# VectorE's attention as a hardware loop of eight trips, with ring slots freed by two VectorE operations

## The chip, the cores and the metric

The kernel runs on one core of one Trainium2 chip. The metric is the device time in microseconds (us) of one execution; times are medians of the fast ones among several executions. Each execution is labelled fast or slow. Slow ones take 444 to 447 us here, and one execution of the kernel before took 888.3 us; they are left out wherever two kernels are compared.

## The reference

It is one decode step of a transformer block with adaptive layer norm, batch 8, one new token per sequence. Attention has 32 query heads on 4 key/value heads, a cache of 8192 positions and head size 128. A gated MLP (1024 to 3584 to 1024) follows.

```python
mod = (_silu(c) @ w_mod).reshape(8, 6, 1, -1)          # sa, ca, ga, sb, cb, gb
h = _layernorm(x) * (1 + ca) + sa
q = (h @ wq).reshape(B, 1, Hq, Dh).transpose(0, 2, 1, 3)
scores = einsum('bhqd,bhkd->bhqk', q, repeat(k_cache)) * Dh ** -0.5
o = einsum('bhqk,bhkd->bhqd', softmax(scores), repeat(v_cache))
x = x + ga * (o.reshape(B, 1, Hq * Dh) @ wo)
h = _layernorm(x) * (1 + cb) + sb
gate, up = h @ W_gate, h @ W_up
return x + gb * ((gate * (gate > 0) * up) @ W_down)
```

The key and value caches are 134 MB of the 185.6 MB that have to be read. Each of these bytes has to be read once, so the reading itself is the natural limit.

## The kernel before

Everything from HBM goes through one ring in SBUF of 128 KB per partition. K and V of one attention step (two of the 32 batch-and-group pairs) take 4 MB each, so four such loads fill the ring: K m, V m, K m+1, V m+1. SyncE issues the loads in a fixed order, each as soon as the readers of what it overwrites are done. A small recorder turns declared reads and writes into semaphore waits.

```python
def pump():
    while stream:
        key, src, n = stream[0]
        lo = cursor[0] if cursor[0] + n <= RING else 0
        if P.unread("arena", lo, lo + n):
            return
        ...
        P.op("sp", lambda e, dst=dst, src=src: e.dma_start(dst, src), writes=[slot_r(lo, lo + n)], dma=True,
             own=("v", key[1] % 2) if key[0] == "v" else None)
```

One attention step: VectorE transposes K in 8 parts (`kt_part`), TensorE multiplies (`qk_part`), VectorE finds the row maxima and folds the previous step's output, ScalarE takes the exponential, VectorE transposes P (`p_turn`), TensorE multiplies by V (`pv`). `qk_part` also declares a read of K's slot that it does not need, so a K slot is freed by TensorE; a V slot is freed by `pv`, TensorE again.

```python
def kt_part(m, e8):
    ...
    P.op("dve", lambda e: e.transpose(ktb[:, to:to + QE].bitcast(dt.uint32), arena[:, lo:lo + QE].bitcast(dt.uint32)),
         reads=[slot_r(lo, lo + QE)], writes=[R("kt", to, to + QE)])

def qk_part(m, e8):
    ...
    P.op("pe", fns, reads=[R("kt", to, to + QE), R("qpad", m % 2, m % 2 + 1), slot_r(place["k", m] + e8 * QE, ...)],
         writes=[bank(b)])

def fold(m, i):
    if m < 0:
        if i == 3:
            P.op("dve", lambda e: e.memset(om[:], 0.0), writes=[R("om")])
        return
    ...
for m in range(M):                     # M = 16
    P.trip = m // 2
    for e8 in range(8):
        kt_part(m, e8)
        qk_part(m, e8)
        if e8 == 5:
            rowmax(m, 0)
    make_qpad(m + 2)
    fold(m - 1, 0); fold(m - 1, 1)     # (joined lines)
    rowmax(m, 1)
    spread(m)
    fold(m - 1, 2)
    headmax(m)
    expo(m)
    fold(m - 1, 3)
    fold_pe(m - 1)
    ...
    p_turn(m)
    pv(m)
```

TensorE's part is already a hardware loop of 8 trips of two steps. Since the body of the loop is the same code in each trip, it cannot wait for ever growing counts; instead, each semaphore that it waits on is counted down by a fixed step at the end of a trip. VectorE's part is written out 16 times.

```python
with nc.Fori(0, len(self.trips), engines=(mybir.EngineType.PE,)):
    for p, limit in zip(self.trips[1], self.limit, strict=True):
        ...
        body(p, want)
    for s, v in self.step.items():
        e.wait_ge(sems[s], v).then_inc(sems[s], -v)
```

## Time and profile before

| What | Value |
|---|---|
| time, fast runs | 437.57 to 437.83 us |
| span of the profiled run | 436.2 us |
| bytes moved, mean rate | 185.79 MB, 426 GB/s |
| VectorE busy, instructions | 263.0 us (60%), 373 |

The page of the kernel before: its span, its busy times, the DMA rows of its 40 slices (tenths of busy time, then GB/s) and the DMA queues. Queue q1 carries the loads that SyncE issues; q8 and q14 carry instructions that engines fetch.

```profile
span 436.2 us, 4054 instructions
...
PE 273.5 (63%) x1697; PEld 124.0 (28%) x1697; DVE 263.0 (60%) x373; ACT 30.7 (7%) x65; POOL 20.9 (5%) x79
...
DMA  9999999999999999999999999999999999999995
GB/s 376 421 457 431 433 433 431 430 433 433 433 433 433 433 433 433 433 433 433 433 433 433 433 433 433 433 433 433 433 433 430 433 433 433 441 429 434 427 421 224
DMA packets 6939, 185.79 MB, mean 426 GB/s; under 512 B 816, under 2 KB 912, under 8 KB 1168
...
q1 hardware_dynamic: 6848, 185.63, 98.8%
q8 instruction: 6, 0.10, 0.1%
...
q14 instruction: 5, 0.04, 0.0%
```

The DMA row is 9 until the last slice, and the rate stays at 430 to 433 GB/s through the attention: the DMA engines that move data do not run dry there. (A 9 only says 90% or more; the steady rate says more.) Every compute engine is idle for a third of the time or more. The place to look for an effect is therefore whether a load is ever issued too late.

The groups of the page, K's transposes (count, busy us, mean ns; then VectorE's idle time just before them and what ended it), and the issues of the K and V loads (count, size, median us from issue to landing):

```profile
L539 DVE STREAM_TRANSPOSE kt<-arena 128x1024 uint32<-128x1024 uint32 x128 | 148.5, 1214 | 40.5 <-DMA arena<-in_A_k_cache_dram 37.9
...
arena<-in_A_k_cache_dram SPq DMA_DIRECT2D x16, 4096.0 KB, 27.5
arena<-in_A_v_cache_dram SPq DMA_DIRECT2D x16, 4096.0 KB, 25.6
```

VectorE waits 37.9 us for K to land, in 16 steps: 2.4 us a step of room. A load lands some 26 us after its issue though its transfer takes 9.7 us, so nearly two others are queued ahead of it.

SyncE's timeline before (start, duration of the issue, both in us):

```profile
73.23 0.33 SPq L343 DMA_DIRECT2D arena<-in_A_k_cache_dram  x1
85.56 0.33 SPq L343 DMA_DIRECT2D arena<-in_A_v_cache_dram  x1
93.25 0.33 SPq L343 DMA_DIRECT2D arena<-in_A_k_cache_dram  x1
```

VectorE's timeline in the same stretch of the kernel before, the two operations that will free slots among them:

```profile
89.15 0.69 DVE L558 TENSOR_REDUCE negm<-ps 128x1 f32<-128x512 f32 x1 [0.24 <-PE ps L550]
...
95.04 0.17 DVE L572 SCALAR_TENSOR_TENSOR mjt<-mj,jms 128x16 f32<-128x16 f32 x1
95.14 0.08 DVE L572 DVE_READ_ACCUMULATOR mjt<-mj,jms 128x1 f32 x1
```

### The profile page before, as it was taken

The page shows a single profiled execution, that of the slowest core. Times are in us where ns is not written, and L with a number is a line of the kernel's source. Part 1 is how long each engine was busy: PE and PEld are TensorE (multiplying, and loading weights), DVE is VectorE, ACT ScalarE, POOL GpSimd, SP SyncE. Part 2 cuts the span into 40 slices and gives each one's busy share as a digit, 9 for nine tenths or more (in the row PEclk, how much of TensorE's full clock was granted, in tenths as well). Part 3 has the DMA queues.
Part 4 walks back from the last instruction along what each step waited for, and adds up shares of the span by engine and source line. Part 5 has one row for each costly group of instructions (what it writes and reads, how often), then busy time and mean ns, then how long its engine had stood idle before and what let it go on. Part 6 is the DMA issues. An engine that isn't in the chain of part 4 may idle for free.

```text
span 436.2 us, 4054 instructions
## 1 busy us (share of the span) xinstructions
PE 273.5 (63%) x1697; PEld 124.0 (28%) x1697; DVE 263.0 (60%) x373; ACT 30.7 (7%) x65; POOL 20.9 (5%) x79
## 2 busy tenths in 40 slices
PE   0052447769595866859586775959586684655237
PEld 0021112324242332424233232423233231342015
DVE  0233057778596878778696877859686877332020
ACT  1100020010101011010101101010101101010000
POOL 7000010000000000000000000000000000000000
PEclk9996558698787989787896969879798978868568
DMA  9999999999999999999999999999999999999995
GB/s 376 421 457 431 433 433 431 430 433 433 433 433 433 433 433 433 433 433 433 433 433 433 433 433 433 433 433 433 433 433 430 433 433 433 441 429 434 427 421 224
DMA packets 6939, 185.79 MB, mean 426 GB/s; under 512 B 816, under 2 KB 912, under 8 KB 1168
## 3 DMA queue, kind: packets, MB, share of 16 engines
q1 hardware_dynamic: 6848, 185.63, 98.8%
q8 instruction: 6, 0.10, 0.1%
q10 hardware_dynamic: 80, 0.02, 0.0%
q14 instruction: 5, 0.04, 0.0%
HBM read 185.63 MB, written 0.02 MB: 426 GB/s over the span
## 4 chain that ended last, share of the span: by engine, by line
DMA 38%; PE 33%; DVE 20%; issue 8%; ACT 0%; SPq 0%
DMA arena<-in_A_k_cache_dram 25%; PE ps L594 13%; PE ps L550 12%; DVE kt L539 12%; DMA arena<-in_w_mod_dram 7%; DMA arena<-in_B_W_down_dram 6%; DVE negm L558 4%; PE ps L744 2%; PE ps L694 1%; PE ps L564 1%; PE ps L615 1%; DVE om L609 1%; DVE mj L569 1%; PE ps L725 1%; PE ps L463 1%
## 5 line engine op out<-in xcount | busy, mean ns | idle before, releaser
L539 DVE STREAM_TRANSPOSE kt<-arena 128x1024 uint32<-128x1024 uint32 x128 | 148.5, 1214 | 40.5 <-DMA arena<-in_A_k_cache_dram 37.9
L550 PE MATMUL ps<-kt,qpad 128*128 128x512 bf16 x512 | 122.0, 384 | 10.3 <-DVE kt L539 8.8
L594 PE MATMUL ps<-arena,pT 128*64 128x512 bf16 x512 | 92.0, 538 | 50.9 <-issue 50.9
L594 PEld LDWEIGHTS ps<-arena,pT 128*64 128x64 bf16 x512 | 44.2, 153 | 92.6 <-issue 86.7
L550 PEld LDWEIGHTS ps<-kt,qpad 128*128 128x128 bf16 x512 | 45.6, 97 | 85.2 <-DVE kt L539 29.6
L585 DVE STREAM_TRANSPOSE pT<-prb 64x1024 bf16<-64x1024 bf16 x32 | 39.7, 1239 | 16.8 <-ACT prb L578 16.3
L578 ACT ACTIVATE prb<-ps,bias 128x1024 bf16<-128x1024 f32 x16 | 17.8, 1114 | 286.5 <-DVE mjt L572 286.5
L558 DVE TENSOR_REDUCE negm<-ps 128x1 f32<-128x512 f32 x32 | 22.0, 688 | 11.3 <-PE ps L550 11.1
L532 POOL COPY qpad<-qR 32x32 bf16<-32x32 bf16 x64 | 13.0, 203 | 304.7 <-PE ps L550 252.0
L725 PE MATMUL ps<-arena,hT 128*32 128x448 bf16 x128 | 11.0, 515 | 13.6 <-DMA arena<-in_B_W_gate_dram 6.8
L564 PE MATMUL ps<-identf,negm 128*128 128x128 f32 x32 | 7.8, 326 | 15.6 <-DVE negm L562 15.6
L615 PE MATMUL ps<-jmp,om 128*128 128x16 f32 x34 | 6.7, 273 | 16.9 <-DVE om L609 16.1
L609 DVE SCALAR_TENSOR_TENSOR om<-ps,im,om 128x128 f32<-128x128 f32 x48 | 16.7, 347 | 0.6
L486 PE MATMUL ps<-arena,hT 128*32 128x512 bf16 x64 | 7.2, 631 | 14.1 <-DMA arena<-in_A_wq_dram 14.1
L732 DVE TENSOR_TENSOR kt<-ps,kt 128x448 bf16<-128x448 f32 x2 | 1.2, 620 | 23.5 <-PE ps L725 23.5
L744 PE MATMUL ps<-arena,hmT 128*32 128x256 bf16 x112 | 9.0, 332 | 5.3 <-DMA arena<-in_B_W_down_dram 5.3
L401 DVE CAST cxr<-ps 128x512 bf16<-128x512 f32 x1 | 0.7, 692 | 18.1 <-PE ps L399 18.1
L399 PE MATMUL ps<-cx,rsel 32*128 32x512 bf16 x1 | 0.6, 604 | 17.5 <-DMA cx<-in_c_dram 17.5
L564 PEld LDWEIGHTS ps<-identf,negm 128*128 128x128 f32 x32 | 4.7, 186 | 23.5 <-DVE negm L562 23.5
L496 DVE CAST kt<-ps 128x512 bf16<-128x512 f32 x1 | 0.7, 692 | 17.8 <-PE ps L486 17.8
L615 PEld LDWEIGHTS ps<-jmp,om 128*128 128x128 f32 x34 | 5.1, 188 | 20.3 <-DVE om L609 19.4
L725 PEld LDWEIGHTS ps<-arena,hT 128*32 128x32 bf16 x128 | 4.2, 128 | 20.1 <-DMA arena<-in_B_W_gate_dram 7.2
(89 smaller groups left out, 103.9 us busy)
## 6 DMA issues: line engine op xcount, KB each, us to landing
arena<-in_A_k_cache_dram SPq DMA_DIRECT2D x16, 4096.0 KB, 27.5
arena<-in_A_v_cache_dram SPq DMA_DIRECT2D x16, 4096.0 KB, 25.6
arena<-in_w_mod_dram SPq DMA_DIRECT2D x2, 6144.0 KB, 24.0
arena<-in_A_wq_dram SPq DMA_DIRECT2D x2, 4096.0 KB, 31.1
arena<-in_A_wo_dram SPq DMA_DIRECT2D x2, 4096.0 KB, 26.9
arena<-in_B_W_gate_dram SPq DMA_DIRECT2D x2, 3584.0 KB, 23.6
arena<-in_B_W_up_dram SPq DMA_DIRECT2D x2, 3584.0 KB, 24.6
arena<-in_B_W_down_dram SPq DMA_DIRECT2D x1, 3584.0 KB, 25.5
```

Of the source, the lines that this page charges most:

```text
L532: P.op("pool", lambda e, n=2 * m + Q // 2, Q=Q: e.tensor_copy(qpad[32 * Q:32 * Q + 32, m % 2, :, 24 + 32 * Q:32 + 32 * Q], qR[32 * Q:32 * ...
L539: P.op("dve", lambda e: e.transpose(ktb[:, to:to + QE].bitcast(dt.uint32), arena[:, lo:lo + QE].bitcast(dt.uint32)), reads=[slot_r(lo, lo ...
L550: fns.append(lambda e, t=t, r=r: e.matmul(ps[:, b, :].rearrange("p (c k) -> p c k", k=32), qpad[:, m % 2, t * 2 + r, 24 - 8 * i:152 - 8 * ...
L558: P.op("dve", lambda e: e.tensor_reduce(negm[:, h:h + 1], ps[:, b, :], AX.X, ALU.max, negate=True), reads=[bank(b)], writes=[R("negm", h, ...
L564: P.op("pe", lambda e: e.matmul(ps[:, 4, 0:128], negm[:, 2:3].to_broadcast([128, 128]), identf[:], start=True, stop=True), reads=[R("negm" ...
L578: P.op("act", lambda e: e.activation(prb[:], ps[:, 2 * z:2 * z + 2, :].rearrange("p h n -> p (h n)"), ACT.Exp, bias=bias[:, z:z + 1], scal ...
L585: P.op("dve", lambda e, g=g: e.transpose(pT[64 * g:64 * g + 64, z, :, g, :], prb[64 * g:64 * g + 64, :]), reads=[R("prb"), R("pT", z, z + ...
L594: fns.append(lambda e, t=t: e.matmul(ps[64 * (t % 2):64 * (t % 2) + 64, 5, :].rearrange("p (i d) -> p i d", d=Dh), pT[:, z, t].rearrange(" ...
L609: P.op("dve", lambda e, i=i: e.scalar_tensor_tensor(out=om[:], in0=ps[:, 5, Dh * i:Dh * i + Dh], scalar=im[:, i:i + 1], in1=om[:], op0=ALU ...
L615: P.op("pe", lambda e: e.matmul(ps[:, 6 + z, 0:16], om[:], jmp[:].rearrange("p g j -> p (g j)"), start=True, stop=True), reads=[R("om"), R ...
L725: fns.append(lambda e, w=w, r=kk - r0, kk=kk, h=h, j=j, b0=b0: e.matmul(ps[32 * j:32 * j + 32, b0 + h, 0:H], hT[:, kk, :], w[:, r, j, h, : ...
L744: fns.append(lambda e, w=w, r=k - r0, k=k, i2=i2, j=j: e.matmul(ps[32 * j:32 * j + 32, 4, 0:256], hmT[:, k, 1 - i2:33 - i2], w[:, r, i2, j ...
```

## The change

VectorE's attention becomes a hardware loop of 8 trips too, with its own set of counted-down semaphores. In the recorder, an operation signals only one semaphore, so an operation that another loop waits for cannot also signal SyncE. Hence slots are freed by two operations that no loop waits for in that way: K m by the head maximum's accumulate, V m-1 by the next step's first row maximum. Trips must be alike, so the first step runs the folds on what lies in PSUM (the result is never kept) in place of a memset. K loads get semaphores of their own, two evictions of q swap between ScalarE and VectorE, and `make_qpad` comes later.

```diff
+    LOOPED = ("dve", "pe")
...
-                 trip=self.trip if eng == "pe" else None)
+                 trip=self.trip if eng in self.LOOPED else None)
...
-                with nc.Fori(0, len(self.trips), engines=(mybir.EngineType.PE,)):
...
+        with nc.Fori(0, len(self.trips["pe"]), engines=tuple(kinds[x] for x in self.LOOPED)):
+            for x in self.LOOPED:
+                for p, limit in zip(self.trips[x][1], self.limit[x], strict=True):
+                    ...
+                    body(x, p, want)
+                for s, v in self.step[x].items():
+                    if v:
+                        engines[x].wait_ge(sems[s], v).then_inc(sems[s], -v)
...
-                     own=("v", key[1] % 2) if key[0] == "v" else None)
+                     own=(key[0], key[1] % 2) if key[0] in "kv" else None)
+                if key[0] in "kv":
+                    P.held[key] = (lo, lo + n)
...
-            P.op("pe", fns, reads=[R("kt", to, to + QE), R("qpad", m % 2, m % 2 + 1), slot_r(...)],
+            P.op("pe", fns, reads=[R("kt", to, to + QE), R("qpad", m % 2, m % 2 + 1)],
+        def free(*keys):
+            return [slot_r(*P.held.pop(key)) for key in keys if key in P.held]
...                                                                         (rowmax)
-                 reads=[bank(b)], writes=[R("negm", h, h + 1)])
+                 reads=[bank(b)] + (free(("v", m - 1)) if h == 0 else []), writes=[R("negm", h, h + 1)])
...                                                                         (headmax)
-                 reads=[R("mj"), R("jms")], writes=[R("mjt"), R("bias", z, z + 1)])
+                 reads=[R("mj"), R("jms"), R("qpad", z, z + 1)] + free(("k", m)), writes=[...])
...                                                                         (fold)
-            if m < 0:
-                if i == 3:
-                    P.op("dve", lambda e: e.memset(om[:], 0.0), writes=[R("om")])
-                return
```

More of the change, by code (lines that the diff above doesn't have):

```diff
@@ L28, in __init__ @@
         self.trip = None
+        self.held = {}
     def _split(self, name, lo, hi):
@@ L76, in op @@
                 s[2], s[3] = i, []
-        o = dict(eng=eng, fns=fns, deps=deps, dma=None, own=own, own_wait=own_wait,
-                 trip=self.trip if eng == "pe" else None)
+        o = dict(eng=eng, fns=fns, writes=list(writes), deps=deps, dma=None, own=own, own_wait=own_wait,
+                 trip=self.trip if eng in self.LOOPED else None)
         if dma:
@@ L87, in unread @@
     def unread(self, name, lo, hi):
-        return any(s[2] is not None and not s[3] for s in self.segs.get(name, []) if s[0] < hi and s[1] > lo)
+        return any(a < hi and b > lo for a, b in self.held.values()) or any(s[2] is not None and not s[3] for s in self.segs.get(name, []) if s[0] < hi and s[1] > lo)
     def plan(self):
@@ L118, in plan @@
             for d in o["waits"]:
-                self.ops[d]["for"].add("pe" if o["eng"] == "pe" else "eng")
-        trips = self.trips = {}
+                self.ops[d]["for"].add((o["eng"], o["trip"] is not None))
+        self.trips = {x: {} for x in self.LOOPED}
         for o in self.ops:
             if o["trip"] is not None:
-                trips.setdefault(o["trip"], []).append(o)
-        if trips:
+                self.trips[o["eng"]].setdefault(o["trip"], []).append(o)
+        for trips in self.trips.values():
             for at in zip(*[trips[t] for t in sorted(trips)], strict=True):
                 assert len({len(o["fns"]) for o in at}) == 1
-                if any(o["for"] for o in at):
-                    for o in at:
-                        o["for"].add("eng")
+                both = set().union(*[o["for"] for o in at])
+                for o in at:
+                    o["for"] = both
         count, dmas = {}, 0
@@ L139, in plan, with count_down @@
             elif o["for"]:
-                assert len(o["for"]) == 1, (o["eng"], o["fns"], o["for"])
+                own = {x for x, loop in o["for"] if loop}
+                assert not own or {x for x, loop in o["for"]} == own and len(own) == 1, (o["eng"], o["writes"], o["for"])
                 o["inc"] = True
-                o["sem"] = (next(iter(o["for"])), o["eng"])
+                o["sem"] = (own.pop() if own else "eng", o["eng"])
                 count[o["sem"]] = o["val"] = count.get(o["sem"], 0) + 1
-        if not trips:
-            return
+        self.base, self.step, self.limit = {}, {}, {}
+        for x in self.LOOPED:
+            self.count_down(x, [self.trips[x][t] for t in sorted(self.trips[x])])
+    def count_down(self, x, trips):
         n = len(trips)
-        self.base, self.step, self.limit = {}, {}, [{} for _ in trips[0]]
-        for x in self.ENGINES:
-            sem = ("pe", x)
-            need = [[max([self.ops[d]["val"] for d in o["waits"] if self.ops[d]["sem"] == sem], default=0) for o in trips[t]]
-                    for t in range(n)]
+        base, step, limit = self.base.setdefault(x, {}), self.step.setdefault(x, {}), self.limit.setdefault(x, [{} for _ in trips[0]])
+        for p in self.ENGINES:
+            sem = (x, p)
+            need = [[max([self.ops[d]["val"] for d in o["waits"] if self.ops[d]["sem"] == sem], default=0) for o in trip]
+                    for trip in trips]
             last = [max(max(need[t]) for t in range(u + 1)) for u in range(n)]
@@ L154, in plan, with emit, body @@
                 continue
-            step = last[-1] - last[-2]
-            assert step > 0 and all(last[u] == last[-1] - step * (n - 1 - u) for u in range(n)), (x, last)
-            self.step[sem], self.base[sem] = step, last[0] - step
+            by = last[-1] - last[-2]
+            assert all(last[u] == last[-1] - by * (n - 1 - u) for u in range(n)), (x, p, last)
+            step[sem], base[sem] = by, last[0] - by
             top = 0
             for at in range(len(trips[0])):
-                v = max(need[t][at] - self.base[sem] - t * step for t in range(n))
+                v = max(need[t][at] - base[sem] - t * by for t in range(n))
                 if v > top:
-                    self.limit[at][sem] = top = v
-            assert top == step
-    def emit(self, eng, e, sems, nc=None):
-        known, off, looped = {}, {}, False
-        def body(o, want):
+                    limit[at][sem] = top = v
+            assert top == by, (x, p, top, by)
+    def emit(self, nc, engines, sems):
+        state = {x: ({}, {}) for x in engines}
+        def body(x, o, want):
+            e = engines[x]
             for s, v in sorted(want.items(), key=str):
@@ L180, in body, with straight @@
                 ins.then_inc(sems[o["sem"]], 1)
-        for o in self.ops:
-            if o["eng"] != eng:
-                continue
-            if o["trip"] is not None:
-                if looped:
-                    continue
-                looped = True
-                for s, v in self.base.items():
+        def straight(x, ops):
+            known, off = state[x]
+            for o in ops:
+                want = {}
+                for d in o["waits"]:
+                    p = self.ops[d]
+                    want[p["sem"]] = max(want.get(p["sem"], 0), p["val"])
+                new = {}
+                for s, v in want.items():
+                    if known.get(s, 0) < v:
+                        known[s] = v
+                        new[s] = v - off.get(s, 0)
+                body(x, o, new)
@@ L190, in emit @@
+        after = {}
+        for x in engines:
+            mine = [i for i, o in enumerate(self.ops) if o["eng"] == x]
+            inside = [i for i in mine if self.ops[i]["trip"] is not None]
+            after[x] = [self.ops[i] for i in mine if inside and i > inside[-1]]
+            straight(x, [self.ops[i] for i in mine if not inside or i < inside[0]])
+            if inside:
+                for s, v in self.base[x].items():
                     if v > 0:
-                        e.wait_ge(sems[s], v).then_inc(sems[s], -v)
+                        engines[x].wait_ge(sems[s], v).then_inc(sems[s], -v)
@@ L192, in emit @@
                     elif v < 0:
-                        e.sem_inc(sems[s], -v)
-                with nc.Fori(0, len(self.trips), engines=(mybir.EngineType.PE,)):
-                    for p, limit in zip(self.trips[1], self.limit, strict=True):
-                        want = dict(limit)
-                        if p["own_wait"] is not None:
-                            want[p["own_wait"]] = 16
-                        body(p, want)
-                    for s, v in self.step.items():
-                        e.wait_ge(sems[s], v).then_inc(sems[s], -v)
@@ L202, in emit @@
-                for s, v in self.step.items():
-                    off[s] = self.base[s] + v * len(self.trips)
-                    known[s] = off[s]
-                continue
-            want = {}
-            for d in o["waits"]:
-                p = self.ops[d]
-                want[p["sem"]] = max(want.get(p["sem"], 0), p["val"])
-            new = {}
-            for s, v in want.items():
-                if known.get(s, 0) < v:
-                    known[s] = v
-                    new[s] = v - off.get(s, 0)
@@ L215, in emit @@
-            body(o, new)
+                        engines[x].sem_inc(sems[s], -v)
+        kinds = dict(dve=mybir.EngineType.DVE, pe=mybir.EngineType.PE)
+        with nc.Fori(0, len(self.trips["pe"]), engines=tuple(kinds[x] for x in self.LOOPED)):
+            for x in self.LOOPED:
+                for p, limit in zip(self.trips[x][1], self.limit[x], strict=True):
+                    want = dict(limit)
+                    if p["own_wait"] is not None:
+                        want[p["own_wait"]] = 16
+                    body(x, p, want)
+                for s, v in self.step[x].items():
+                    if v:
+                        engines[x].wait_ge(sems[s], v).then_inc(sems[s], -v)
@@ L218, in start_loads_first @@
+        for x in self.LOOPED:
+            known, off = state[x]
+            for s, v in self.step[x].items():
+                known[s] = off[s] = self.base[x][s] + v * len(self.trips[x])
+            straight(x, after[x])
 def start_loads_first(nc, n):
@@ L311, in bass_adaLN_cond__gqa_block_cached__glu_gated_reglu__decode_kernel @@
             sems[("pe", x)] = E(nc.semaphore("p_" + x))
-        for i in range(2):
-            sems[("v", i)] = E(nc.semaphore("v_%d" % i))
+        for x in ("act", "pool", "dve", "pe"):
+            sems[("dve", x)] = E(nc.semaphore("v_" + x))
+        for t in "kv":
+            for i in range(2):
+                sems[(t, i)] = E(nc.semaphore("%s_%d" % (t, i)))
         def R(t, lo=0, hi=1):
@@ L516, in bass_adaLN_cond__gqa_block_cached__glu_gated_reglu__decode_kernel @@
                     dst = qR[:, u, :, 4 * jh:4 * jh + 4].rearrange("p (b g) j -> p b g j", g=G)
-                    if jh == 0:
+                    if jh == 1:
                         P.op("dve", lambda e, s=src, d=dst: e.tensor_copy(d, s), reads=[bank(5 + jh)],
@@ L539, in kt_part @@
             P.op("dve", lambda e: e.transpose(ktb[:, to:to + QE].bitcast(dt.uint32), arena[:, lo:lo + QE].bitcast(dt.uint32)),
-                 reads=[slot_r(lo, lo + QE)], writes=[R("kt", to, to + QE)])
+                 reads=[slot_r(lo, lo + QE)], writes=[R("kt", to, to + QE)], own_wait=("k", m % 2) if e8 == 0 else None)
         def qk_part(m, e8):
@@ L552, in qk_part @@
                         kv[:, :, t, :, r], start=(i == 0 and t == 0 and r == 0), stop=(i == 3 and t == 1 and r == 1)))
-            P.op("pe", fns, reads=[R("kt", to, to + QE), R("qpad", m % 2, m % 2 + 1), slot_r(place["k", m] + e8 * QE, place["k", m] + e8 * QE + QE)],
+            P.op("pe", fns, reads=[R("kt", to, to + QE), R("qpad", m % 2, m % 2 + 1)],
                  writes=[bank(b)])
+        def free(*keys):
+            return [slot_r(*P.held.pop(key)) for key in keys if key in P.held]
         def rowmax(m, h):
@@ L573, in headmax @@
                                                          op1=ALU.mult, accum_out=bias[:, z:z + 1]),
-                 reads=[R("mj"), R("jms")], writes=[R("mjt"), R("bias", z, z + 1)])
+                 reads=[R("mj"), R("jms"), R("qpad", z, z + 1)] + free(("k", m)), writes=[R("mjt"), R("bias", z, z + 1)])
         def expo(m):
@@ L600, in fold @@
         def fold(m, i):
-            if m < 0:
-                if i == 3:
-                    P.op("dve", lambda e: e.memset(om[:], 0.0), writes=[R("om")])
-                return
             if i == 0:
@@ L639, in bass_adaLN_cond__gqa_block_cached__glu_gated_reglu__decode_kernel @@
                     rowmax(m, 0)
-            make_qpad(m + 2)
             fold(m - 1, 0)
@@ L646, in bass_adaLN_cond__gqa_block_cached__glu_gated_reglu__decode_kernel @@
             headmax(m)
+            make_qpad(m + 2)
             expo(m)
@@ L659, in bass_adaLN_cond__gqa_block_cached__glu_gated_reglu__decode_kernel @@
             fold(M - 1, i)
+        P.held.clear()
         fold_pe(M - 1)
@@ L758, in bass_adaLN_cond__gqa_block_cached__glu_gated_reglu__decode_kernel @@
         P.plan()
-        for name, e in (("sp", nc.sync), ("act", nc.scalar), ("pool", nc.gpsimd), ("dve", nc.vector), ("pe", nc.tensor)):
-            P.emit(name, e, sems, nc)
+        P.emit(nc, dict(sp=nc.sync, act=nc.scalar, pool=nc.gpsimd, dve=nc.vector, pe=nc.tensor), sems)
         start_loads_first(nc, 3)
```

## The prediction

> **What bounds it now.** The DMA engines. In the page's 40 slices the DMA row reads 9 everywhere but the last, at 430 to 433 GB/s through the attention. 185.79 MB at 433 GB/s is 429.1 us of a 436.2 us span. The other 7 us are a slower first slice (376 GB/s) and the end (224 GB/s in the last slice), where the last weights are multiplied after they land. [...] VectorE is busy 60%, PE 63%. The chain of waits names DVE 20% and PE 33%, but those steps only free ring slots; they leave no gap in the DMA row.
>
> **What changes.** VectorE's 16 attention steps become 8 trips. The work is the same, but step 0 now runs four folds on stale data (0.31 + 3 x 0.35 us) in place of a 0.17 us memset: +1.2 us, once. Each trip adds some counted-down waits and a branch[...]. TensorE's larger loop shows no cost in this trace: its QK matmuls follow PV without idle time at a trip end (104.09 us) as inside a trip (85.5). VectorE has room: the groups table shows 37.9 us of waiting for K's DMA before 16 steps, 2.4 us a step. Two evictions of q swap engines (0.89 and 0.79 us), with 3.1 us of idle VectorE before K 0 lands at 62.0.
>
> **Where it touches the critical path: when slots come free.** By SyncE's timeline, V loads are issued when PV ends (85.56, 104.12) and K loads when the last QK ends (93.25, 111.81). Now V waits for the next step's first row maximum (ends 89.84, 108.4): 4.3 us later; K for the head maximum's accumulate (95.2, 113.8): 2 us later. Loads are queued far ahead: issue to landing is 25.6 us (V) and 27.5 (K) for a transfer of 9.7 us (4.19 MB at 433). At a V issue moved to 89.9, V 1 lands at about 91 and K 2 at 100.6: 10.7 us of work is still queued, against 15 before. So no bubble. Later loads (up, second gate, down) still wait for TensorE, with 11 us and more in hand.
>
> **Predicted: 437.7 us, no change (before 437.83).** Range 437.0 to 438.8. Faster by over 2%: 0.01; within 2%: 0.97; slower by over 2%: 0.02.
>
> **What would show each step.**
> - DMA row still 9 in 39 slices, 430 to 433 GB/s in attention, span within 1 us of 436.2.
> - V's issue-to-landing falls from 25.6 to about 21.3 us, K's from 27.5 to about 25.4; SyncE's waits name VectorE's row maximum and accumulate in place of PE.
> - VectorE busy rises by 1 to 2 us; its idle time before the K transposes falls slightly at most.
> - VectorE's instruction count stays about 375; instruction-queue bytes fall a little.
>
> **What would make it wrong.** If the branch causes an instruction fetch behind 4 MB loads and costs VectorE 5 us or more a trip, VectorE falls behind, the 10.7 us of queue is eaten and the DMA row shows gaps. Or if a wait counted for both steps of a trip is stricter than before, so that VectorE waits for TensorE or ScalarE in each step, the idle time before the K transposes would be for PE, not DMA. If V's issue comes 15 us later than before, gaps follow. Set-up at the start or end could shift the time by tenths of a us either way.

Two passages are cut from it where marked, as no trace or run of this case shows what they said: a ceiling for the DMA rate, and a time for a branch with the estimate for a trip that rested on it. Neither enters the forecast as a term. It came to 437.7 us, no change from the 437.83 us of before: the added work and the branches were taken to fit into VectorE's 2.4 us of waiting a step.

## The result

| | before | changed |
|---|---|---|
| median of the fast runs | 437.66 us | 436.93 us |
| fast runs | 437.57 to 437.83 us | 436.86 to 437.21 us |
| median of all six runs | 437.77 us | 436.96 us |
| span of the profiled run | 436.2 us | 435.7 us |

The ratio of the changed kernel to the one before is 0.9984, with a 95% interval of 0.9968 to 1.0. (Ratios are the mean time of one kernel's fast runs over that of the other's of the same rounds, so they are not quite the ratio of the medians quoted.) The fast runs of the two do not overlap, and 0.7 us lies between their medians (0.8 us between the medians of all runs, the figure that the expectations below use).

The page of the changed kernel, the lines that answer to those shown of before:

```profile
span 435.7 us, 4112 instructions
...
PE 276.6 (63%) x1697; PEld 126.3 (29%) x1697; DVE 265.2 (61%) x376; ACT 30.7 (7%) x65; POOL 20.8 (5%) x79
...
DMA  9999999999999999999999999999999999999995
GB/s 367 430 454 432 433 433 432 431 433 433 433 433 433 433 433 433 431 433 433 433 433 433 433 433 433 433 431 433 433 433 433 433 433 433 429 428 436 428 423 241
DMA packets 6937, 185.77 MB, mean 426 GB/s; under 512 B 816, under 2 KB 912, under 8 KB 1168
...
q8 instruction: 6, 0.10, 0.1%
...
q14 instruction: 3, 0.02, 0.0%
...
L560 DVE STREAM_TRANSPOSE kt<-arena 128x1024 uint32<-128x1024 uint32 x128 | 149.4, 1217 | 36.9 <-DVEq L179 32.4
...
arena<-in_A_k_cache_dram SPq DMA_DIRECT2D x16, 4096.0 KB, 25.1
arena<-in_A_v_cache_dram SPq DMA_DIRECT2D x16, 4096.0 KB, 20.8
```

SyncE's timeline and, below it, its longest waits (waited for: total us, times, longest) in the changed kernel:

```profile
75.44 0.33 SPq L362 DMA_DIRECT2D arena<-in_A_k_cache_dram  x1
90.15 0.33 SPq L362 DMA_DIRECT2D arena<-in_A_v_cache_dram  x1
95.54 0.33 SPq L362 DMA_DIRECT2D arena<-in_A_k_cache_dram  x1
```

```profile
SPq L362 <- DVE negm L583: 204.4, 15, 14.4
SPq L362 <- DVE mjt L597: 94.8, 16, 19.2
```

The V load is issued at 90.15 instead of 85.56 and the K load at 95.54 instead of 93.25. Issue to landing shrinks by about the same amounts, so the landing itself does not move (this V load lands at 110.28 before and at 110.34 now): the DMA row stays full. The idle time before the K transposes falls by 3.6 us in all (40.5 to 36.9, waits of every kind). Its releaser is now VectorE's own sequencer (DVEq), because the wait for K's semaphore has become an instruction of its own that also counts the semaphore down; the thing awaited is still K's landing: the transposes of the second K start at 81.50 us, 0.14 us after that landing (81.36), against 0.02 us after it in the kernel before (81.31 and 81.29).

One line differs that bears on the small gain: q14 has 3 packets instead of 5, each of 8 KB by the trace. (VectorE's program is shorter now: two steps stand in it instead of sixteen, so there are fewer instructions to fetch.) To see what that could do, the end of each load was read from the trace. The trace holds 16 reports for each load, as many as the core has DMA engines; they are read here as one from each, when its share is down. The kernel's readers wait for all 16, so for them a load lands with its slowest engine. The trace shows it: of the second K's reports in the kernel before, the first is at 79.63 us and the last at 81.29, and VectorE starts on this K at 81.31. How far the engines are behind the first to report, for some loads (us; sorted, so a place in the list is a rank and not a fixed engine):

```
                      load landed at   the three slowest engines, us behind the first
before                71.63            0.38 0.58 1.68
   q14 fetch at 79.3  81.29            1.05 1.56 1.66
                      207.10           0.87 1.46 1.64
   q14 fetch at 207.2 216.98           1.47 1.65 1.84 (and the 0.87 is gone)
                      323.35           1.46 1.64 1.72
   q14 fetch at 330.3 334.00           1.46 1.64 2.68
                      433.24 (last)    1.62 1.67 2.52
changed               81.36            0.72 1.61 1.77
   q14 fetch at 85.5  91.02            1.18 1.63 1.77
                      332.95           1.04 1.60 1.68
                      432.43 (last)    1.64 1.65 1.73
```

In the kernel before, one engine goes back by about 0.95 us at each of the fetches at 207.2 and 330.3. At the last one that engine is already among the slowest, so the load, and all that follow, land about 1 us later. The two fetches not in the table (173.8 and 292.4) have counterparts at 177.5 and 292.6 in the changed kernel, and in every experiment, however many instructions VectorE has; they are probably another engine's. The changed kernel has only one of the three others, and its engine never becomes the slowest. The last load lands 0.81 us earlier. Of this, 0.55 us show in the spans of the two profiled runs (436.21 and 435.67): in the changed one the result is stored 1.63 us after that landing, in the other 1.38 us after it.

### The profile page after: what moved, and what is told of

Same layout as the page of the kernel before. It is cut to its first block, busy times and chain, and to the rows that moved or that the text cites. A ratio compares the mean times of both kernels' runs of the same rounds, so it can differ in the third digit from the quotient of the medians.

```text
span 435.7 us, 4112 instructions
## 1 busy us (share of the span) xinstructions
PE 276.6 (63%) x1697; PEld 126.3 (29%) x1697; DVE 265.2 (61%) x376; ACT 30.7 (7%) x65; POOL 20.8 (5%) x79
## 4 chain that ended last, share of the span: by engine, by line
PE 47%; DVE 20%; issue 13%; DMA 6%; ACT 0%
PE ps L619 21%; PE ps L571 18%; DVE kt L560 9%; DMA arena<-in_B_W_down_dram 6%; DVE negm L583 5%; PE ps L766 2%; PE ps L589 2%; PE ps L636 2%; PE ps L716 1%; DVE om L630 1%; DVE mj L594 1%; PE ps L747 1%; DVE mjt L597 1%; DVE negm L587 1%; DVE kt L706 0%
## 5 line engine op out<-in xcount | busy, mean ns | idle before, releaser
L560 DVE STREAM_TRANSPOSE kt<-arena 128x1024 uint32<-128x1024 uint32 x128 | 149.4, 1217 | 36.9 <-DVEq L179 32.4
L619 PE MATMUL ps<-arena,pT 128*64 128x512 bf16 x512 | 93.0, 543 | 50.8 <-issue 50.8
L747 PE MATMUL ps<-arena,hT 128*32 128x448 bf16 x128 | 12.5, 576 | 10.9 <-DMA arena<-in_B_W_up_dram 5.3
L630 DVE SCALAR_TENSOR_TENSOR om<-ps,im,om 128x128 f32<-128x128 f32 x51 | 17.7, 347 | 0.7
## 6 DMA issues: line engine op xcount, KB each, us to landing
arena<-in_A_k_cache_dram SPq DMA_DIRECT2D x16, 4096.0 KB, 25.1
arena<-in_A_v_cache_dram SPq DMA_DIRECT2D x16, 4096.0 KB, 20.8
```

Of the source, the lines that this page charges most:

```text
L619: fns.append(lambda e, t=t: e.matmul(ps[64 * (t % 2):64 * (t % 2) + 64, 5, :].rearrange("p (i d) -> p i d", d=Dh), pT[:, z, t].rearrange(" ...
L630: P.op("dve", lambda e, i=i: e.scalar_tensor_tensor(out=om[:], in0=ps[:, 5, Dh * i:Dh * i + Dh], scalar=im[:, i:i + 1], in1=om[:], op0=ALU ...
L747: fns.append(lambda e, w=w, r=kk - r0, kk=kk, h=h, j=j, b0=b0: e.matmul(ps[32 * j:32 * j + 32, b0 + h, 0:H], hT[:, kk, :], w[:, r, j, h, : ...
```

## The experiments

Two questions are open: where the 0.7 us come from, and whether the prediction's two reserves (2.3 us a step on VectorE, 10.7 us of queued transfers) are real. All runs below gave correct results. Ten kernels ran. The changed kernel was not run again beside them. The kernel before was, in each of the three sessions, and the medians of its fast runs were 437.66, 437.52 and 437.61 us, so times of different sessions can be compared to about 0.2 us.

### e1_unrolled: the loop taken back, the rest kept

```diff
-    LOOPED = ("dve", "pe")
+    LOOPED = ("pe",)
...
-                    if known.get(s, 0) < v:
+                    if o["own_wait"] == s:
+                        new[s] = v
+                    elif known.get(s, 0) < v:
```

> The changed kernel with VectorE's attention written out again (no loop on VectorE); slots are still freed by VectorE's two operations, the folds and evictions are those of the changed kernel. Theory A (the 0.8 us comes from fewer instruction fetches, because each fetch puts one of the 16 DMA engines behind and a load has landed only when its slowest engine has): 5 packets on queue q14 again, not 3; the loads' landing spread (first to last engine) grows again to 2.2 to 2.7 us by the end; time 437.3 to 438.0 us. Theory B (it comes from when slots are freed or in what order loads are issued): 436.9 us, as the changed kernel. VectorE's idle time before the K transposes stays near 37 us.

Measured: 437.70 us median of the fast runs (437.61 to 437.90; one slow run, 445.89), ratio to before 1.0002 (0.9989 to 1.0014). That is the time of the kernel before, not of the changed one. The interval overlaps that of the changed kernel (0.9968 to 1.0); what tells the two apart is that none of the fast runs overlap. The page of this run:

```profile
span 436.6 us, 4071 instructions
...
q14 instruction: 5, 0.04, 0.0%
...
L562 DVE STREAM_TRANSPOSE kt<-arena 128x1024 uint32<-128x1024 uint32 x128 | 148.2, 1213 | 41.9 <-DVEq L179 40.9
```

The five fetches are back, and the last load's engines are spread by 2.73 us. So freeing the slots with VectorE, the later issues, the extra folds and the swapped evictions together give nothing. The gain comes with the loop. The idle time before the K transposes (41.9 us) was 5 us above what was expected; nothing rests on it.

### e2_unrolled_padded and e2_looped_padded: the same extra work, fetched or not

Both e1 and the changed kernel get 32 one-element memsets at the end of each step (here and in e3, e6 and e8 a small tile `spare` is added too, not shown):

```diff
             p_turn(m)
             pv(m)
+            for i in range(32):
+                P.op("dve", lambda e, i=i: e.memset(spare[0:1, i:i + 1], 0.0))
```

> As e1, plus 32 one-element memsets at the end of each of 16 steps, 512 VectorE instructions of some 60 ns, about 2 us a step, inside the 2.3 us of waiting. Theory A: 4 more q14 packets than e1 (9), so the slowest DMA engine is put behind further: 0.3 to 2 us slower than e1, 437.8 to 439.8 us. Theory B and a rival that only VectorE's busy time counts: the same as e1.

> The changed kernel (looped) with the same 32 memsets a step: the same VectorE work as e2_unrolled_padded but no instructions fetched again. Theory A: 3 or 4 q14 packets, 436.7 to 437.3 us, so 0.5 us or more faster than its written-out twin. If VectorE's work itself counted: equal to the twin.

Measured: written out 441.29 us (441.20 to 442.30), ratio 1.0091 (1.0076 to 1.0106). Looped 437.20 us (436.84 to 439.02), ratio 0.9998 (0.9985 to 1.0012). The twins execute the same 888 VectorE instructions (32 memsets took 0.40 us, not the 2 us expected: each lasts 59 ns by the groups of both runs, but they overlap, 12.5 ns apiece), and lie 4.1 us apart; the slower one has the smaller busy time. First the lines of the written-out page, then of the looped one:

```profile
span 439.8 us, 4583 instructions
...
PE 275.2 (63%) x1697; PEld 123.8 (28%) x1697; DVE 269.3 (61%) x888; ACT 30.7 (7%) x65; POOL 20.9 (5%) x79
...
q14 instruction: 9, 0.07, 0.0%
```

```profile
span 435.5 us, 4624 instructions
...
PE 276.6 (64%) x1697; PEld 125.0 (29%) x1697; DVE 271.6 (62%) x888; ACT 30.7 (7%) x65; POOL 20.8 (5%) x79
...
q14 instruction: 3, 0.02, 0.0%
```

512 written-out instructions made exactly four more packets on q14 than in e1, so one packet is 128 VectorE instructions (8 KB). The cost was above what was expected (0.3 to 2 us over e1; measured 3.6). The reports of the 16 engines show why. At the fetches at 163.3, 219.9, 261.9, 313.6 and 360.4 the slowest engine's lag goes 1.80 to 2.81, 2.70 to 3.59, 3.61 to 4.49, 4.41 to 5.37, 5.29 to 6.30. It steps by 0.9 to 1.0 us each time while the second slowest stays at 1.8. A packet's record does not name its DMA engine, but by these lags VectorE's fetches hit the same one every time; once it is the slowest, each costs the whole kernel 0.9 us.

### e8_head128 and e8_head256: one and two more fetches in the looped kernel

128 or 256 one-element memsets at the head of VectorE's program, where it idles 18 us:

```diff
+        for i in range(256):                     # or 128
+            P.op("dve", lambda e, i=i: e.memset(spare[0:1, i:i + 1], 0.0))
         P.op("pe", lambda e: e.matmul(ps[:, 6, :], rsel[:]...
```

> The changed kernel with 128 one-element memsets (12.5 ns each, 1.6 us in all) at the head of VectorE's program, where it idles 18 us. Each 128 VectorE instructions are 8 KB, so one more fetch (q14: 4). In e2_unrolled_padded each VectorE fetch put the same DMA engine behind by 0.9 us. In the changed kernel VectorE's one fetch leaves that engine at about 1.05 us behind the first, while the slowest is at 1.65 to 1.8. Theory A': one more fetch brings it to about 2.0: 0.1 to 0.3 us slower than the changed kernel, 436.9 to 437.3. Rival (every fetch costs its 0.9 us in the time): 437.8.

> As e8_head128 with 256 memsets: two more fetches (q14: 5, as in the kernel before). Theory A': the engine ends about 2.9 us behind the first, 1.0 to 1.2 us more than the slowest of the changed kernel: 437.8 to 438.2 us, as slow as the kernel before or slower, although VectorE is still looped. Theory B (slots, order): 436.9.

Measured: with 128, 437.04 us median (436.73 to 439.60, two of the six runs near 439), against 436.93 without. With 256, 437.88 us (437.78 to 438.02), as slow as the kernel before (437.52 in the same session). Their ratios to before, both 1.0008 (0.9983 to 1.0033 and 0.9995 to 1.0021), do not tell them apart, because of those two runs; the medians, the spreads and the pages do. The lines of the two pages, 128 first:

```profile
span 435.6 us, 4240 instructions
...
q14 instruction: 4, 0.03, 0.0%
```

```profile
span 436.5 us, 4368 instructions
...
q14 instruction: 6, 0.04, 0.0%
```

The first extra fetch is nearly free, since it only uses up the lag that VectorE's DMA engine had in hand (in the changed kernel it was about 1.04 us behind the first at 332.95, and the slowest 1.68). The second costs 0.8 us. (The sixth packet of the second page is one of 96 bytes; five of 8 KB lie in its span, as expected.) The looped kernel with five such fetches is no faster than the written-out one.

Set the profiled runs side by side, and the span less the spread of the last load (from the first of its 16 reports to the last) lies between 433.7 and 434.0. Left out are e7 (slow), e4 and e6, in which the DMA queue runs empty, and e3, in which the difference is 435.8: there the second load of w_mod landed at 34.04 us, against 31.8 to 33.3 in the runs of the table, and all later loads came later with it; why is open.

| run | q14 fetches of 8 KB | spread of the last load, us | span, us | difference |
|---|---|---|---|---|
| before | 5 | 2.52 | 436.2 | 433.7 |
| changed | 3 | 1.73 | 435.7 | 434.0 |
| e1_unrolled | 5 | 2.73 | 436.6 | 433.9 |
| e2_unrolled_padded | 9 | 6.11 | 439.8 | 433.7 |
| e2_looped_padded | 3 | 1.78 | 435.5 | 433.7 |
| e8_head128 | 4 | 1.85 | 435.6 | 433.8 |
| e8_head256 | 5 | 2.84 | 436.5 | 433.7 |
| e5_v_with_k (below) | 3 | 1.97 | 435.8 | 433.8 |

In these eight runs the engines of a load drift apart while loads are queued without a pause: the spread of the reports was 0.6 to 2.2 us at the first large load and 1.7 to 6.1 us at the last (0.59 and 2.52 before, 0.75 and 1.73 in the changed kernel), and it did not close while the queue stayed full. In e4 (below), once VectorE made gaps, it fell from 1.6 us (139 us into the run) to 0.5 us (171 us).

### e7_trips4: four trips of four steps on both engines

```diff
-            P.trip = m // 2
+            P.trip = m // 4
```

> The changed kernel with 4 trips of 4 steps, on both engines: half the branches, twice the loop's code. Theory A: the time follows the number of fetches, and TensorE's larger loop (twice as many matmuls) may need more: if q8 or q14 packets rise, up to 1 us slower than 436.9 us; if they stay, 436.9. A rival that a branch costs time on the critical path: faster than 436.9 by something. VectorE's idle time before the K transposes within 1 us of 36.9.

Measured: fast runs 436.92 to 437.46 us (median 437.21), ratio 0.9988 (0.9975 to 1.0001). Two of the seven runs were slow, the profiled one among them, so the times of its profile are not compared. Half the branches made nothing faster. The result does not say more than that.

### e3_extra2 and e4_extra5: how much room VectorE has

One more reduce at the end of each step, of 2048 and of 5120 elements:

```diff
             p_turn(m)
             pv(m)
+            P.op("dve", lambda e: e.tensor_reduce(spare[:, 0:16], identf[:, None, :].to_broadcast([128, 16, 128]), AX.X, ALU.add))
```

> The changed kernel with one more reduce of 2048 elements (about 2.15 us) on VectorE at the end of each step. The prediction's claim that VectorE has 2.3 us of room a step: the time stays within 0.3% of 436.9; the idle time before the K transposes falls from 36.9 us to under 8. If VectorE were on the critical path: 16 x 2.15 = 34 us slower.

> The same with 5120 elements (about 5.4 us) a step, 3.1 us over the room. Now VectorE paces the attention: its step is 22.5 us instead of 19.4, 50 us of lag by the end of the attention, part of it hidden by the loads that are queued ahead: 460 to 485 us, with gaps in the DMA row. With K always landed before VectorE wants it, the idle time before a K transpose at a trip's start less that inside a trip is the price of the branch: under 0.5 us.

Measured: with 2048 elements (2.29 us each by the trace, where 2.15 was the estimate; 37 us in all) 436.91 us, median of four fast runs from 436.76 to 439.18, ratio 0.9985 (0.9966 to 1.0004): no change. With 5120 elements (5.49 us, estimated at 5.4) 471.96 us, ratio 1.0818 (1.0756 to 1.0879). The idle time before the K transposes, from the pages of e3 and e4:

```profile
L561 DVE STREAM_TRANSPOSE kt<-arena 128x1024 uint32<-128x1024 uint32 x128 | 148.6, 1215 | 7.8 <-DVEq L179 4.2
```

```profile
L561 DVE STREAM_TRANSPOSE kt<-arena 128x1024 uint32<-128x1024 uint32 x128 | 147.6, 1212 | 2.9 <-DVEq L179 2.9
```

The first addition ate the room and nothing else; the second went past it and the time rose by 35 us. (The profiled run of e3 took 439.18 us, about 2 us more than the other three. The trace shows them lost before the attention: the second load of w_mod lands at 34.04 us, against 31.95 in the changed kernel. Its idle time, not its span, is used here.) In e4 VectorE never waits for K after the first step, so a branch that held it up would lie open. VectorE's timeline in e4, the first K transposes of four steps in a row, two of them at a trip's start:

```profile
195.29 6.87 DVE L561 STREAM_TRANSPOSE kt<-arena 128x1024 uint32<-128x1024 uint32 x6
...
217.33 6.87 DVE L561 STREAM_TRANSPOSE kt<-arena 128x1024 uint32<-128x1024 uint32 x6
...
239.37 6.87 DVE L561 STREAM_TRANSPOSE kt<-arena 128x1024 uint32<-128x1024 uint32 x6
...
261.41 6.87 DVE L561 STREAM_TRANSPOSE kt<-arena 128x1024 uint32<-128x1024 uint32 x6
```

They are 22.04 us apart each time, with no idle time before any, branch or none (under 0.5 us was allowed for it). A branch costs VectorE nothing that shows here, where a 5.49 us reduce comes just before each; what it costs without one was not measured.

### e5_v_with_k and e6_v_late: how late a slot may be freed

In e5 V's slot is freed with K's, at the head maximum's accumulate. In e6 it is freed by a tiny memset after the P transposes; the next K load stands behind it in SyncE's order. The row maximum no longer frees anything.

```diff
-                 reads=[bank(b)] + (free(("v", m - 1)) if h == 0 else []), writes=[R("negm", h, h + 1)])
+                 reads=[bank(b)], writes=[R("negm", h, h + 1)])
...                                                                         (e5, headmax)
-  ... + free(("k", m)), writes=[R("mjt"), R("bias", z, z + 1)])
+  ... + free(("v", m - 1), ("k", m)), writes=[R("mjt"), R("bias", z, z + 1)])
...                                                                         (e6, after p_turn)
+            P.op("dve", lambda e: e.memset(spare[0:1, 0:1], 0.0), reads=free(("v", m - 1)))
```

> The changed kernel with V's slot freed by the head maximum's accumulate, with K's, instead of by the row maximum: V's loads issued 5.4 us later (about 95.5 instead of 90.15). By then K 2 (landing at 100.6) is what is left in the queues: 5 us. Prediction's queue argument: still no gap, 436.7 to 437.4 us; V's issue-to-landing falls from 20.8 to about 15.5 us. If when slots come free mattered in this region: slower by some us.

> V's slot freed only after the step's P transposes, 9.1 us later than in the changed kernel (about 99.3 at the first), with the K load held behind it in SyncE's order. Only 1.3 us of K 2's transfer is left then, less than a load's start-up: gaps of 0.5 to 2 us a step in the DMA row, 445 to 465 us. If the loads could still be started without a gap: 437.

Measured: e5 437.06 us, ratio 0.9978 (0.9949 to 1.0006). V's issue to landing is 15.8 us and there is still no gap, by the lines of its page:

```profile
GB/s 367 430 451 432 433 433 429 434 430 433 433 436 433 433 433 436 431 433 433 433 433 433 433 433 433 433 431 433 436 433 433 433 433 433 426 428 438 430 418 240
...
arena<-in_A_v_cache_dram SPq DMA_DIRECT2D x16, 4096.0 KB, 15.8
```

e6 453.04 us, ratio 1.0342 (1.0309 to 1.0375). SyncE's timeline in e6 and the DMA rows of its page:

```profile
100.70 0.33 SPq L363 DMA_DIRECT2D arena<-in_A_v_cache_dram  x1
101.07 0.43 SPq L363 DMA_DIRECT2D arena<-in_A_k_cache_dram  x1
120.77 0.33 SPq L363 DMA_DIRECT2D arena<-in_A_v_cache_dram  x1
```

```profile
DMA  9999999999999999999999999999899999999995
GB/s 414 409 369 409 434 420 444 429 411 391 405 425 437 425 376 428 423 399 402 434 420 396 431 382 443 379 435 446 347 446 417 431 388 422 402 437 422 429 416 230
```

The first V load shown is issued 2.4 us before the K load ahead of it, the last one queued, lands (103.06 by the trace), and it still lands without a gap. The next one, with 1.7 us left, lands 11.9 us after the load ahead of it instead of the usual 9.7. From there on the rate swings between 347 and 447 GB/s: the queue runs out again and again, though the DMA row reads 9 almost everywhere. Gaps of this size show in the GB/s row alone.

So the reserve is a fact, and the traces say how much of it is needed. What counts is how long before the landing of the load ahead of it a load is issued. For the first V load of this stretch that was 15 us in the kernel before and 10.5 us in the changed one. In e5 it is 5.4 to 6.4 us for the V loads of the attention, and each lands 9.7 us after the one ahead. In e6, of ten loads issued with 1.7 to 3.1 us left, six land over 1 us late (10.8 to 12.1 us after the one ahead). In e4 the V loads from 158 us on are issued with next to nothing left (0.3 us too late to 0.2 us before) and land 12.0 to 12.8 us after the one ahead: a load that starts on an empty queue loses 2.4 to 3.1 us here (the start-up of e6's expectation). As e5's 5.4 us were enough, the prediction's 10.7 us were about twice what would have done.

## Why the prediction was right

- **The DMA engines bound it, no change.** Right: 433 GB/s in nearly every slice of the attention before and after. The measured median, 436.96 us (436.93 of the fast runs), lies at the very low end of the range (437.0, to its precision); the forecast, 437.7, was 0.7 us too high, and the last point of this list says why.
- **VectorE's added work is hidden.** Right, and tested: busy time rose by 2.2 us (263.0 to 265.2, predicted 1 to 2), and e3 hides another 37 us. The idle time before the K transposes fell from 40.5 to 36.9 us.
- **A branch shows no cost.** Not contradicted: the prediction read it from TensorE's loop, and e4 shows no difference between VectorE's steps with and without a branch (22.04 us each). No run here isolates what a branch alone takes. Nor does it bring a fetch in each trip: by the lags, one VectorE fetch in all fell into the changed kernel's run.
- **Slots come free later, without a bubble.** Right in size: V 4.6 us and K 2.3 us later at the first (predicted 4.3 and 2); issue to landing 20.8 and 25.1 us (predicted 21.3 and 25.4). e5 and e6 bracket where this would have failed.
- **Instruction-queue bytes fall a little.** Right as a count (q14 from 5 to 3 packets), and here the prediction stopped short. It did not see that this is the part of the change that reaches the time. The last load lands with the slowest of 16 DMA engines, a VectorE fetch of 8 KB puts one of them back by 0.9 us, and the kernel before had one fetch more than that engine had room for. That is worth 0.7 us. The forecast of no change stood because this effect is small, not because it was weighed.

Shown by runs: the loop, not the freeing, gives the 0.7 us (e1, by fast runs that do not overlap); instructions fetched, not work done, cost it (the e2 pair); added fetches take it away again (e8). Read from the trace but not tried by itself: that a load's landing follows its slowest engine. Open: why a fetch whose record shows 0.31 us puts its DMA engine back by 0.9 us, and what the first 1.7 us of spread would cost to remove. They appear at the load that follows a 16 KB fetch on q8 at 36 us; another one at 71 us puts a second engine nearly as far back (1.56 us at 81.29). That queue is probably TensorE's: e7, whose TensorE loop is twice as long, has 7 packets on it instead of 6, the one more at 115 us, in the attention. No run was made to test its cost. No version tried beats the changed kernel clearly.

## What to carry to other kernels

Before costing a change in a kernel whose DMA row is full, ask only how late it makes the issue of a load and how much work is still queued at that moment (here 5.4 us of it were enough, and 1.7 to 3.1 us were not always); engine time inside the waiting was free until it was used up (37 us more on VectorE cost nothing, 88 us cost 35). Instruction fetches were transfers here too: each of VectorE's put one DMA engine back by 0.9 us, and since a load landed with its slowest engine, a shorter program on an engine with room gained 0.7 us, where 37 us of work on that engine made no difference. A loop that stays short is a way to get there, but expect tenths of a per cent (0.2% here).
